# A drain of GpSimd between the third and the fourth half tile, and a count loaded behind the tiles in the text

## The chip, the cores and the metric

The kernel runs on one core of one Trainium2 chip. The metric is the device time of one execution in microseconds (us). Every run is one execution of the whole program; three runs of the kernel before were timed, and one more was taken with the hardware profiler.

## What is computed

`x` is [4, 3072, 256] in float32. The reference takes a Fourier transform over the sequence and then over the channels and keeps the real part. A channel mix follows on each token and its predecessor, and then a gated squared-ReLU layer; the 12288 tokens that come out go through a mixture of eight experts, of which each token takes one:

```python
X = np.fft.fft(np.fft.fft(x, axis=1), axis=2).real
xk = mu_k * X + (1 - mu_k) * X_prev;  xr = mu_r * X + (1 - mu_r) * X_prev
y = sigmoid(xr @ w_r) * (np.maximum(xk @ w_k, 0) ** 2 @ w_v)          # then 12288 tokens of 256
e_idx = argmax(y @ w_gate); gate_w = softmax(y @ w_gate)[e_idx]; eom = sigmoid(y @ w_output_gate)
for e in range(8):
    out[e_idx == e] = gate_w * eom[e] * (np.maximum(y @ w1[e], 0) @ w2[e])
```

## The kernel before

The first two thirds of the kernel (up to about 830 us of the span) do the Fourier transforms and the gated layer in 24 blocks of 512 tokens. For each block, GpSimd issues four indirect transfers that write the tokens' numbers into one list for each expert (`lists`, line 491).

Then comes the expert stage. It works in tiles of 256 tokens that all take the same expert, and in half tiles of 128 for what is left over of an expert. `make_plan` works out on the chip which expert each tile takes and where its list starts, and writes it into the table `plan`. `pipeline` walks a fixed sequence: 3 early tiles, 22 tiles and 5 half tiles (`HALVES`). A tile is gathered by an indirect transfer of GpSimd (`gather`, line 621, into `xg`), goes through the first product (`m1`, tile `hps`) and the second (`m2`, tile `o`), is scaled by ScalarE (line 706), and is written out by an indirect transfer of GpSimd (line 707, `out<-o,ix`): two stores for a tile, one for a half tile. GpSimd's queue is in order, so an instruction that waits there holds up every later transfer of GpSimd.

Behind the fixed sequence stands a branch (`tc.If(extra > 0)`, line 895) for inputs whose experts are so unevenly filled that more tiles are needed. Each of the five engines loads the count `extra` from `plan` into a register (line 890) and takes the branch by itself. In the profiled execution nothing is left over and every engine jumps over the code of the further tiles. On the path that is jumped to, each engine raises the semaphores that the skipped code would have raised; GpSimd does it for its eight transfer semaphores with one instruction, named INC_SWDGE_SEM in the profile. Then come the end of the program (line 926 in the profile): SyncE waits for all semaphores, GpSimd has a DRAIN, all engines meet at a barrier, the semaphores are cleared, and they meet again.

The instructions are not issued in the order of the text alone: a scheduler sets the order within each engine from dependencies and priorities, and `follow` adds an edge to it that carries no semaphore (`NoSync`).

Of the kernel before, what the change touches and what calls it, by code (L numbers as in the profile page):

```python
# [25 lines left out]
NTILE = NT // TT + E - 1  # L26
EARLY = 3
MORE = [22, 26, 31, 38, NTILE]
HALVES = 5
CAP = NT + TT  # L30
ROW = 265
FAR = 1 << 20
# [13 lines left out]
def constants():  # L46
# [28 lines left out]
    desc = np.broadcast_to(E - e8, (128, 4, E))  # L75
    base = np.broadcast_to(e8 * CAP, (128, 4, E))
    tri = np.broadcast_to((e8[:, None] >= e8[None, :]).astype(float), (128, E, E))
# [18 lines left out]
def moe_kernel(ctx: ExitStack, tc: tile.TileContext, x, mu_k, mu_r, wk2, wv2, wr2, wg, wo, w1, w2,  # L96
               c_f, c_t, c_m, c_r, c_s, c_id, out):
    nc = tc.nc
    PE, ACT, DVE, POOL, SP = nc.tensor, nc.scalar, nc.vector, nc.gpsimd, nc.sync
# [4 lines left out]
    def tt(o, a, b, op, eng=None):  # L104
        return (eng or DVE).tensor_tensor(out=o, in0=a, in1=b, op=op)  # L105

    def stt(o, a, s, b, op0, op1, **kw):
        return DVE.scalar_tensor_tensor(out=o, in0=a, scalar=s, in1=b, op0=op0, op1=op1, **kw)  # L108
# [26 lines left out]
    zeros = dram.tile([16, 4096], F32, name="zeros")  # L135
    lists = dram.tile([E * CAP + TT, 2], I32, name="lists")

# [14 lines left out]
    def follow(i, earlier, kind, reason):  # L152
        for k in earlier:
            tc.add_manual_dep(i.ins, k.ins.name, mybir.DependencyInfo(kind, mybir.DependencyReason.DATA), reason=reason)

    def load_later(o, i):
        follow(SP.dma_start(o, i), raws[1:2], mybir.DependencyClass.NoSync, "the first groups come first")
# [13 lines left out]
    def clear_lists():  # L171
        zero = bp.tile([128, 512], F32, name="zero", tag="lt", bufs=1)
        POOL.memset(zero, 0.0)
        load_later(zeros.rearrange("a (p d) -> (a p) d", d=512), zero)
        per = (E * CAP + TT) // (6 * 128) * 2
        far = bp.tile([128, per], I32, name="far", tag="lt", bufs=1)
# [239 lines left out]
    def tail_steps(n, vps, rs):  # L416
# [73 lines left out]
        for u in range(4):  # L490
            i = POOL.indirect_dma_start(lists[:, :], bass.IndirectOffsetOnAxis(ap=pi[:, u:u + 1], axis=0),  # L491
                                        cid[:, n, u], None,
                                        bounds_check=E * CAP - 1, oob_is_err=False)
            for k in done:
# [79 lines left out]

    c1 = {}
    weights, xtile, meta, index, chunks, regs = {}, {}, {}, {}, {}, {}
    hq, outs, stores = {}, {}, []

    def open_c1():
        sa.close()  # L580
# [17 lines left out]
    def width(t):  # L598
        return 2 if t < NTILE else 1

    def read_plan(t):
        why = "experts and list starts are clamped to their ranges, flags are 0 or 1"
        regs[t] = [nc.values_load_multi_w_load_instructions(
            c1["plan"][0:1, t, i:i + 1], engines=[mybir.EngineType.SP], min_val=0, max_val=hi,
            skip_runtime_bounds_check_because=why)[1][0] for i, hi in ((0, E - 1), (1, 1), (2, E * CAP))]

    def gather(t):
        if t < 0:
            start = (t + EARLY) * TT
            src = lists[start:start + TT]  # L610
        else:
            read_plan(t)
            src = lists[bass.ds(regs[t][2], 128 * width(t)), :]
        ix = bp.tile([128, 2, 2], I32, tag="ix", name="ix", bufs=8)
        after_scatters(SP.dma_start(ix[:, 0:width(t)], src.rearrange("(p u) o -> p u o", u=width(t))))
        index[t] = ix
        place[t] = len(place)
        xg = c1["xg"][place[t] % 4]
        for u in range(width(t)):
            nr = NT if t >= 0 else NT - 1024  # L620
            POOL.indirect_dma_start(xg[:, u], None, rows[0:nr],  # L621
                                    bass.IndirectOffsetOnAxis(ap=ix[:, u, 0:1], axis=0),
                                    bounds_check=nr - 1, oob_is_err=False)
# [14 lines left out]
    def split_w(t, c):  # L638
        h, l = weights[t][c // 2]
        k = slice((c % 2) * 512, (c % 2) * 512 + 512)  # L640
        split(h[:, k], l[:, k], c1["raw"][c // 2][:, k])
# [46 lines left out]
    def m2(t, p):  # L688
        if p == 0:
            outs[t] = [pm.tile([128, D], F32, tag="m", name=f"o{u}") for u in range(width(t))]  # L690
        h, l = hq.pop((t, p))
        for u in range(width(t)):
            for a in range(2):
                f = 2 * p + a
                wh, wl = weights[t][2 + f // 4]
                cols = slice((f % 4) * D, (f % 4) * D + D)
                tok = slice(u * 128, u * 128 + 128)
                ps = outs[t][u]
                PE.matmul(ps, h[:, a, tok], wh[:, cols], start=f == 0, stop=False)  # L699
                PE.matmul(ps, l[:, a, tok], wh[:, cols], start=False, stop=False)  # L700
                PE.matmul(ps, h[:, a, tok], wl[:, cols], start=False, stop=f == 7)  # L701
        if p == 3:
            sc, ix = meta.pop(t), index.pop(t)
            o = bp.tile([128, 2, D], F32, tag="t1", name="o", bufs=2)
            for u in range(width(t)):
                ACT.activation(out=o[:, u], in_=outs[t][u], func=ACTF.Copy, scale=sc[:, u])
                i = POOL.indirect_dma_start(out[:, :], bass.IndirectOffsetOnAxis(ap=ix[:, u, 1:2], axis=0),
                                            o[:, u], None, bounds_check=NT - 1, oob_is_err=False)
                for k in stores[-4:]:
                    tc.declare_no_dep(i.ins, k.ins, reason="every token is in one list once: rows are distinct")  # L710
                stores.append(i)
            outs.pop(t)
            weights.pop(t)

# [5 lines left out]
    def make_plan():  # L720
# [44 lines left out]
        DVE.tensor_scalar(lc, lc, float(TT), None, ALU.mult)  # L765
        stt(lc, et, float(CAP), lc, ALU.mult, ALU.add)
        stt(st, et, 0.5, early[:, :, 0:1].to_broadcast([128, NTILE, 1]), ALU.is_lt, ALU.mult)
# [28 lines left out]
        DVE.tensor_scalar(at[:, :, 0:1], cum[:, :, E - 1:E], float(-MORE[0]), 0.0, ALU.add, ALU.max)  # L796
        DVE.tensor_scalar(at[:, :, 1:2], cuh[:, :, E - 1:E], float(-HALVES), 0.0, ALU.add, ALU.max)
        tt(half[:, 0:1, 3:4], at[0:1, :, 0:1], at[0:1, :, 1:2], ALU.add)

    def pipeline(seq, ahead=0):  # L800
        n = len(seq)
        bank = 0
        for t in seq:
            banks[t] = bank = 0 if t < 0 else 1 - bank
        for i in range(ahead, min(3, n)):
            gather(seq[i])
        if not ahead:
            load_w(seq[0], True)
            for c in range(8):
                split_w(seq[0], c)  # L810
            prep_x(seq[0])
            prep_scale(seq[0])

        def needs_w(i):
            return i < n and not (seq[i] < 0)

        if needs_w(1):
            load_w(seq[1])
        steps = [(i, p) for i in range(n) for p in range(4)]
        for g in range(len(steps) + 2):  # L820
            if g < len(steps):
                i, p = steps[g]
                m1(seq[i], p)
            if g >= 2:
                m2(seq[steps[g - 2][0]], steps[g - 2][1])
            if g < len(steps) and i + 1 < n:
                with ExitStack() as es:
                    for k in marks:
                        es.enter_context(tc.issue_after(k.ins))
                    if needs_w(i + 1):  # L830
                        split_w(seq[i + 1], 2 * p)
                        split_w(seq[i + 1], 2 * p + 1)
                    else:
                        weights[seq[i + 1]] = weights[seq[i]]
                    if p == 2:
                        prep_x(seq[i + 1])
                    if p == 3 and seq[i] < 0:
                        prep_scale(seq[i])
                    if p == 2 and seq[i + 1] >= 0:
                        prep_scale(seq[i + 1])  # L840
                if p == 0 and i + 3 < n:
                    gather(seq[i + 3])
                if p == 3 and needs_w(i + 2):
                    load_w(seq[i + 2])
# [41 lines left out]
    for _ in tail:  # L886
        pass
    sb.close()
    make_plan()
    value = lambda i, top, why: nc.values_load(  # L890
        c1["plan"][0:1, i:i + 1, 3:4].rearrange("p a b -> p (a b)"), min_val=0, max_val=top,
        skip_runtime_bounds_check_because=why)
    extra = value(NTILE, NTILE + E, "what is left of sums that add up to at most NTILE and E")
    pipeline(list(range(-EARLY, MORE[0])) + list(range(NTILE, NTILE + HALVES)), EARLY)
    with tc.If(extra > 0):
        total = value(0, NTILE, "a sum of rounded counts that add up to at most NT")
        halves = value(NTILE + 1, E, "at most one half tile of each expert")
        with ExitStack() as rest:
            for a, b in zip(MORE, MORE[1:]):
                rest.enter_context(tc.If(total > a))  # L900
                pipeline(list(range(a, b)))
        with tc.If(halves > HALVES):
            pipeline(list(range(NTILE + HALVES, NTILE + E)))

# [25 lines left out]
```

## Time and profile before

| what | value |
|---|---|
| time, median of 3 runs | 1190.78 us (1190.38 to 1191.68) |
| the profiled execution's own time | 1189.58 us |
| span of the profiled execution, first to last instruction | 1187.8 us |
| TensorE busy | 1135.6 us (96% of the span) |
| GpSimd busy | 228.4 us (19%) |

The span is shorter than the execution's own time by 1.78 us, which lie outside the first and the last instruction. The busy times count instructions that an engine executes; register loads, branches, semaphore instructions and drains, which an engine's sequencer carries out, are not among them and are found only by their line. In the names of the views "POOLq" is GpSimd's queue (sequencer) and "POOL" the engine behind it, and so for the others.

### The profile page before, as it was taken

The numbers are of one execution on the slowest core, as the hardware profiler recorded it, in microseconds if no ns is written. First come the engines' busy times: TensorE is split into PE (matmuls) and PEld (weight loads), VectorE is DVE, ScalarE is ACT, GpSimd is POOL, SyncE is SP. The second block draws the span as 40 slices with busy tenths as digits, with TensorE's granted clock in tenths as the row PEclk, the third lists the DMA queues.
The fourth block names the chain that finished last, engine by engine and source line by source line (L and its number), as shares of the span: only waits on it lengthen the run. The fifth ranks groups of instructions, "written<-read, shape, count | busy, mean of one in ns | idle before, by whom it ended". The sixth has DMA issues, their size and how long they took to land.

```text
span 1187.8 us, 19728 instructions
## 1 busy us (share of the span) xinstructions
PE 1135.6 (96%) x6743; PEld 971.6 (82%) x6743; DVE 892.6 (75%) x2032; ACT 775.3 (65%) x1611; POOL 228.4 (19%) x228
## 2 busy tenths in 40 slices
PE   5499999999999999999999999999999999999994
PEld 1477888888888888888887888877999999999994
DVE  1899898578869768768857877776677777777782
ACT  3577777567777667767756666855376676667671
POOL 1000111111100111111111111123342433343220
PEclk9699999999999999999999999999999999999998
DMA  8753551214432215324100000202234133441580
GB/s 275 235 183 126 157 160 55 88 57 130 128 126 81 81 54 144 76 65 128 48 28 29 28 28 19 90 20 55 88 119 147 47 113 109 118 124 38 156 246 13
DMA packets 63176, 119.17 MB, mean 100 GB/s; under 512 B 14299, under 2 KB 41181, under 8 KB 62297
## 3 DMA queue, kind: packets, MB, share of 16 engines
q1 hardware_dynamic: 51015, 91.62, 25.2%
q0 software_dynamic: 9296, 16.76, 4.6%
q10 hardware_dynamic: 2754, 9.44, 2.8%
q8 instruction: 55, 0.90, 0.4%
q14 instruction: 56, 0.46, 0.2%
HBM read 116.43 MB, written 46.57 MB: 137 GB/s over the span
## 4 chain that ended last, share of the span: by engine, by line
PE 87%; DMA 3%; DVE 3%; issue 3%; ACT 1%; SPq 1%; POOL 0%; POOLq 0%; ACTq 0%
PE v L252 8%; PE v L253 7%; PE v L254 7%; PE psk L252 7%; PE psk L253 7%; PE psk L254 7%; PE hps L254 4%; PE hps L253 4%; PE hps L252 4%; PE o L701 4%; PE o L700 4%; PE o L699 4%; PE ps L364 4%; PE ps L252 2%; PE psr L252 2%
## 5 line engine op out<-in xcount | busy, mean ns | idle before, releaser
L491 POOL DMA_INDIRECT lists<-cid,pi x96 | 100.9, 1051 | 683.9 <-DVE pi L488 622.3
L108 DVE SCALAR_TENSOR_TENSOR t<-psk,t 128x512 f32<-128x512 f32 x192 | 132.3, 689 | 62.5 <-ACT t L530 60.3
L530 ACT ACTIVATE t<-psk 128x512 f32<-128x512 f32 x192 | 114.3, 597 | 97.6 <-PE psk L254 84.8
L105 DVE TENSOR_TENSOR ql<-t,qh 128x512 fp32r<-128x512 f32 x192 | 132.4, 690 | 37.0 <-ACT qh L102 35.2
L252 PE MATMUL psk<-kh,wkh 128*128 128x512 f32 x384 | 156.6, 408 | 2.2 <-DVE t L108 1.2
L252 PE MATMUL v<-qh,wvh 128*128 128x512 f32 x384 | 153.7, 400 | 0.2 <-ACT qh L102 0.2
L253 PE MATMUL v<-qh,wvl 128*128 128x512 f32 x384 | 152.0, 396 | 0.0
L253 PE MATMUL psk<-kh,wkl 128*128 128x512 f32 x384 | 151.6, 395 | 0.0
L254 PE MATMUL psk<-kl,wkh 128*128 128x512 f32 x384 | 151.1, 394 | 0.0
L254 PE MATMUL v<-ql,wvh 128*128 128x512 f32 x384 | 150.2, 395 | 0.0
L102 ACT ACTIVATE qh<-t 128x512 fp32r<-128x512 f32 x192 | 120.7, 629 | 42.3 <-DVE t L108 35.4
L684 ACT ACTIVATE hh<-hps 128x512 fp32r<-128x512 f32 (+1 forms) x120 | 67.4, 562 | 107.6 <-PE hps L254 89.9
L108 DVE SCALAR_TENSOR_TENSOR hl<-hps,hh 128x512 fp32r<-128x512 f32 (+1 forms) x120 | 77.5, 646 | 73.7 <-ACT hh L684 63.1
L621 POOL DMA_INDIRECT xg<-rows,ix x55 | 61.5, 1119 | 183.0 <-PE hps L254 48.1
L252 PEld LDWEIGHTS psk<-kh,wkh 128*128 128x128 f32 x384 | 72.5, 189 | 17.6 <-DVE t L108 1.6
L254 PEld LDWEIGHTS v<-ql,wvh 128*128 128x128 f32 x384 | 72.3, 188 | 17.2 <-DVE ql L105 0.4
L254 PEld LDWEIGHTS psk<-kl,wkh 128*128 128x128 f32 x384 | 72.3, 188 | 16.7
L252 PEld LDWEIGHTS v<-qh,wvh 128*128 128x128 f32 x384 | 72.3, 188 | 15.3 <-ACT qh L102 0.9
L253 PEld LDWEIGHTS psk<-kh,wkl 128*128 128x128 f32 x384 | 72.6, 189 | 14.2
L253 PEld LDWEIGHTS v<-qh,wvl 128*128 128x128 f32 x384 | 72.5, 189 | 14.3
L108 DVE SCALAR_TENSOR_TENSOR mx<-xt,omu,mx 128x512 f32<-128x512 f32 x96 | 71.9, 749 | 6.3 <-ACT mx L402 5.3
L105 DVE TENSOR_TENSOR wlb<-raw,whb 128x512 fp32r<-128x512 f32 x112 | 73.3, 686 | 2.5 <-ACT whb L102 0.8
(219 smaller groups left out, 3102.5 us busy)
## 6 DMA issues: line engine op xcount, KB each, us to landing
raw<-in_moe_w SPq DMA_DIRECT2D x112, 512.0 KB
rows<-row SPq DMA_DIRECT2D x24, 530.0 KB
raw<-scr SPq DMA_DIRECT2D x24, 512.0 KB
out<-zeros SPq DMA_DIRECT2D x48, 256.0 KB
xs<-in_x SPq DMA_DIRECT2D x24, 480.0 KB
scr<-e ACTq DMA_DIRECT2D x18, 480.0 KB
tb<-in_c_t SPq DMA_DIRECT2D x20, 256.0 KB
scr<-xs POOLq DMA_DIRECT2D x6, 480.0 KB
```

What stands on the lines that cost most here:

```text
L102: return ACT.activation(out=o, in_=i, func=ACTF.Copy, scale=scale)
L105: return (eng or DVE).tensor_tensor(out=o, in0=a, in1=b, op=op)
L108: return DVE.scalar_tensor_tensor(out=o, in0=a, scalar=s, in1=b, op0=op0, op1=op1, **kw)
L252: PE.matmul(ps, ah, bh, start=start, stop=False)
L253: PE.matmul(ps, al, bh, start=False, stop=False)
L254: return PE.matmul(ps, ah, bl, start=False, stop=stop)
L364: PE.matmul(ps[:, a * 128:a * 128 + 128], f[:, a, c, par * 128:par * 128 + 128], tb[:, a, c], start=c == 0, stop=c == 1)
L491: i = POOL.indirect_dma_start(lists[:, :], bass.IndirectOffsetOnAxis(ap=pi[:, u:u + 1], axis=0), cid[:, n, u], None, bounds_check=E * CAP ...
L530: ACT.activation(out=t, in_=ps, func=ACTF.Relu)
L621: POOL.indirect_dma_start(xg[:, u], None, rows[0:nr], bass.IndirectOffsetOnAxis(ap=ix[:, u, 0:1], axis=0), bounds_check=nr - 1, oob_is_err ...
L684: marks[:] = [last, ACT.activation(out=h, in_=ps, func=ACTF.Relu), stt(l, ps, 0.0, h.bitcast(F32), ALU.max, ALU.subtract)]
L699: PE.matmul(ps, h[:, a, tok], wh[:, cols], start=f == 0, stop=False)
```

## The change

A DRAIN of GpSimd is issued behind the store of the third of the five half tiles (`DRAIN_AT` is its number). Two edges hold it in its place in the order: it follows that store, and the stores of the fourth and fifth half tile follow it. The lines that load the count `extra` move behind the call of `pipeline` in the text.

```diff
+DRAIN_AT = NTILE + HALVES - 3
...
-    hq, outs, stores = {}, {}, []
+    hq, outs, stores, drains = {}, {}, [], []
...
                 stores.append(i)
+                if drains and t > DRAIN_AT:
+                    follow(i, drains[:1], mybir.DependencyClass.NoSync, "what is written from here on is retired at the end")
+            if t == DRAIN_AT:
+                drains.append(POOL.drain())
+                follow(drains[0], stores[-width(t):], mybir.DependencyClass.NoSync, "this much is retired first")
...
     make_plan()
+    pipeline(list(range(-EARLY, MORE[0])) + list(range(NTILE, NTILE + HALVES)), EARLY)
     value = lambda i, top, why: nc.values_load(
...
     extra = value(NTILE, NTILE + E, "what is left of sums that add up to at most NTILE and E")
-    pipeline(list(range(-EARLY, MORE[0])) + list(range(NTILE, NTILE + HALVES)), EARLY)
     with tc.If(extra > 0):
```

GpSimd's queue at the end of the expert stage, before: the last gather, the stores of the five half tiles, and the load of the count with its branch (drains are not among the rows that this listing shows).

```order
L621 DMA xg_8449<-rows,ix 128x265 [waits DMAHW0_49,DVE_49,PE_49]
L707 DMA out<-o,ix 12288x256 [waits DMASW0_49,Activation_49]
L707 DMA out<-o,ix 12288x256 [waits DMASW2_49,DMASW1_49,Activation_49]
L707 DMA out<-o,ix 12288x256 [waits DMASW3_49,Activation_49]
L707 DMA out<-o,ix 12288x256 [waits DMASW5_49,Activation_49]
L707 DMA out<-o,ix 12288x256 [waits DMASW6_49,DMASW4_49,Activation_49]
L890 TENSOR_LOAD plan [waits DVE_49]
L895 COMPARE_AND_BRANCH
```

The same place of GpSimd's queue after the change (line 708 is the store, 897 the load of the count).

```order
L622 DMA xg_8449<-rows,ix 128x265 [waits DMAHW0_49,DVE_49,PE_49]
L708 DMA out<-o,ix 12288x256 [waits DMASW0_49,Activation_49]
L708 DMA out<-o,ix 12288x256 [waits DMASW2_49,DMASW1_49,Activation_49]
L708 DMA out<-o,ix 12288x256 [waits DMASW3_49,Activation_49]
L708 DMA out<-o,ix 12288x256 [waits DMASW5_49,Activation_49]
L708 DMA out<-o,ix 12288x256 [waits DMASW6_49,DMASW4_49,Activation_49]
L897 TENSOR_LOAD plan [waits DVE_49]
L901 COMPARE_AND_BRANCH
```

Nothing that is listed has moved, and the waits are the same: the load of the count stood behind the last store before and stands there now. Between the fourth and the fifth of these rows (the stores of the third and of the fourth half tile) the built program now has the DRAIN, with no wait and no semaphore of its own. Instruction by instruction, that DRAIN is the one difference between the two programs on all five engines.

SyncE's queue at the same place, before: the last loads of weights and the load of the count.

```order
L633 DMA raw_8445<-in_moe_w 128x1024 [waits DMAHW2_49,DVE_49]
L633 DMA raw_8446<-in_moe_w 128x4x256 [waits DMAHW3_49,DVE_49]
L633 DMA raw_8447<-in_moe_w 128x4x256 [waits DMAHW4_49,DMAHW0_49,DVE_49]
L890 TENSOR_LOAD plan [waits DVE_49]
L895 COMPARE_AND_BRANCH
```

It reads the same after the change but for the line numbers, and so do the queues of TensorE, VectorE and ScalarE.

## Rows read from the trace of the kernel before

**Rows 1.** The page: span, and busy time, share and instructions of each engine.

```profile
span 1187.8 us, 19728 instructions
PE 1135.6 (96%) x6743; PEld 971.6 (82%) x6743; DVE 892.6 (75%) x2032; ACT 775.3 (65%) x1611; POOL 228.4 (19%) x228
```

**Rows 2.** Windows at the end: stretch, length, busy us of engines (instructions), clock, DMA share.

```profile
1158.00:1168.00 10.00, 10.00 (x90) 10.00 (x89) 6.21 (x16) 5.17 (x13) 1.96 (x2) 1.00 0.06 21
1168.00:1173.00 5.00, 3.19 (x28) 2.99 (x26) 0.42 (x1) 0.86 (x2) 0.98 (x1) 1.00 0.06 19
1173.00:1175.80 2.80, 0.00 (x0) 0.00 (x0) 0.00 (x0) 0.00 (x0) 0.00 (x0) 1.00 0.13 34
1178.20:1187.80 9.60, 0.00 (x0) 0.00 (x0) 0.00 (x0) 0.00 (x0) 0.00 (x0) 0.50 0.00 0
```

**Rows 3.** Line 895, branch and jumped-to path: count, min/median/max ns, first and last start.

```profile
L895 SPq EVENT_SEMAPHORE  x9: 17/17/17, 1159.7 to 1160.3; - x9
L895 POOLq EVENT_SEMAPHORE  x5: 17/42/43, 1175.2 to 1175.7; - x5
...
L895 POOLq COMPARE_BRANCH  x1: 53/53/53, 1172.3 to 1172.3; - x1
L895 POOLq INC_SWDGE_SEM  x1: 2335/2335/2335, 1175.8 to 1175.8; - x1
```

**Rows 4.** Line 926, the program's end, in three windows.

```profile
L926 SPq EVENT_SEMAPHORE  x7: 27/28/28, 1178.1 to 1178.5; - x7
L926 POOLq DRAIN  x1: 8812/8812/8812, 1178.2 to 1178.2; - x1
...
L926 SPq DRAIN  x2: 7/10/13, 1178.8 to 1178.9; - x2
...
L926 POOLq EVENT_SEMAPHORE  x2: 17/17/17, 1187.0 to 1187.1; - x2
...
L926 POOLq DRAIN  x2: 44/76/107, 1187.2 to 1187.5; - x2
```

**Rows 5.** Line 914, the program's start.

```profile
L914 POOLq INC_SWDGE_SEM  x1: 27/27/27, 0.1 to 0.1; - x1
...
L914 POOLq DRAIN  x1: 188/188/188, 0.3 to 0.3; - x1
```

**Rows 6.** GpSimd's transfers over the span, by tile: count, KB each.

```profile
scr<-xs POOLq DMA_DIRECT2D x6, 480.0 KB
...
lists<-cid,pi POOLq DMA_INDIRECT x96
xg<-rows,ix POOLq DMA_INDIRECT x55
out<-o,ix POOLq DMA_INDIRECT x55
...
scr<-xs POOLq DMA_DIRECT2D x1, 192.0 KB
```

**Rows 7.** Line 890, the load of the count: queue, ns, start.

```profile
L890 SPq TENSOR_LOAD <-plan x1: 273/273/273, 1155.4 to 1155.4; - x1
...
L890 POOLq TENSOR_LOAD <-plan x1: 498/498/498, 1171.7 to 1171.7; - x1
```

**Rows 8.** Timeline of GpSimd: start, us, what, idle before it and its releaser.

```profile
1158.09 0.98 POOL L707 DMA_INDIRECT out<-o,ix  x1 [7.44 <-ACT o L706]
1166.48 0.98 POOL L707 DMA_INDIRECT out<-o,ix  x1 [7.42 <-ACT o L706]
1171.97 0.98 POOL L707 DMA_INDIRECT out<-o,ix  x1 [4.51 <-ACT o L706]
```

**Rows 9.** GpSimd's transfer queue (q0): packets in 1160 to 1162, then in 1174 to 1175.

```profile
q0 software_dynamic: 2, 0.00, 0.1%
...
q0 software_dynamic: 5, 0.01, 5.5%
```

**Rows 10.** Timeline of VectorE behind the third store.

```profile
1158.36 0.69 DVE L105 TENSOR_TENSOR wlb<-raw,whb 128x512 fp32r<-128x512 f32 x1 [0.19 <-ACT whb L102]
...
1163.32 0.42 DVE L108 SCALAR_TENSOR_TENSOR hl<-hps,hh 128x256 fp32r<-128x256 f32 x1
1165.38 0.42 DVE L108 SCALAR_TENSOR_TENSOR hl<-hps,hh 128x256 fp32r<-128x256 f32 x1 [1.63 <-ACT hh L684]
```

**Rows 11.** Lines 491 and 707: GpSimd's indirect transfers, min/median/max ns.

```profile
L491 POOL DMA_INDIRECT lists<-cid,pi x96: 977/979/1576, 125.8 to 844.4; - x96
...
L707 POOL DMA_INDIRECT out<-o,ix x55: 978/1017/1472, 859.8 to 1172.0; - x55
```

## The prediction

> **What bounds the kernel now.** I read the page first. TensorE is busy for 1135.6 of 1187.8 us [rows 1], so over the body of the kernel it is the bound, and GpSimd with 228.4 us is far from it. A change that touches only GpSimd's queue can therefore matter only where TensorE has nothing left to do, and the windows at the end show that place [rows 2]: TensorE is full from 1158 to 1168 (10.00 of 10 us), ends in the next window, and from 1173 to 1187.8 no engine executes anything. These last 15 us or so, 1.2% of the span, are register, branch and semaphore work, which the busy times don't count; so I went on to the lines of the branch, the program's end and the program's start.
>
> The tail reads like this. GpSimd starts the fifth half tile's store at 1171.97 and has written its descriptors after 0.98 us [rows 8]; the last packets of its transfer queue fall in 1174 to 1175 [rows 9]. GpSimd's queue took the branch at 1172.3, and its first instruction at the target starts at 1175.2: five semaphore waits, then INC_SWDGE_SEM at 1175.8 for 2.335 us [rows 3]. At 1178.2 comes its DRAIN, which takes 8.812 us; the barrier follows at 1187.0, and all is over at 1187.8 [rows 4]. SyncE, released at 1178.1, is through its waits and drains by 1178.9 and has nothing to do for the 8 us that follow [rows 4]. So the chain that ends the program runs through one instruction that executes nothing visible.
>
> What does this DRAIN do? All of GpSimd's transfers have landed by 1175, and the engine behind the queue has been empty since 1172.95, so it waits for neither. At the program's start the same two instructions, on the same queue, take 27 ns (INC_SWDGE_SEM) and 188 ns (a DRAIN behind the first fills) [rows 5]; and right after the long DRAIN two more take 44 and 107 ns [rows 4]. What lies between the short ones and the long one is that GpSimd issued 6 + 1 + 96 + 55 + 55 = 213 transfers [rows 6] with no DRAIN among them. My reading, which is an inference, is bookkeeping: each issued transfer leaves an entry that somebody must clear, the DRAIN clears all since the last one, 8.812 / 213 = 41 ns each, and after that there is nothing to clear.
>
> [...]
>
> **The change, part by part.** *The load of the count.* This part does nothing. In the profile of before the load already runs behind the tiles: at 1155.4 us on SyncE, behind its last weight load, and at 1171.7 us on GpSimd, behind its last store [rows 7]. The built order of all five queues is the same before and after. Cost 0; the cover is not needed, since nothing moves.
>
> *The added DRAIN, at its place.* It stands in GpSimd's queue behind the third half tile's store, which starts at 1158.09 and is generated at 1159.07 [rows 8]. Behind it in the queue stand only the fourth store (1166.48), the fifth (1171.97), and the load of the count. Nobody else's work waits for GpSimd any more: the last gather is ahead of it. By the price above it has 6 + 1 + 96 + 55 + 53 = 211 entries to clear, 211 x 41 ns = 8.7 us. If it starts with the store's issue, it ends at 1158.1 + 8.7 = 1166.8; if it must first see the third store land (its last packets fall behind 1160 [rows 9]), at about 1160.5 + 8.7 = 1169.2. I take 1159.07 + 8.7 = 1167.8. The fourth store's data are ready at 1166.2, so that store waits some 1.6 us and is generated by 1169.1. That delay costs nothing: the fifth store can't start before ScalarE has scaled its half tile, which gives 1171.97. The cover is gone if the DRAIN ends later than 1171.97 - 1.28 (one store with its issue) = 1170.7. So the DRAIN may take up to 11.6 us from 1159.07 before it costs anything, and each us beyond is lost one for one.
>
> *The last DRAIN.* It now has two entries to clear, 0.08 us by the price above, and at least the 0.04 to 0.19 us of the short ones. It doesn't give back all of 8.8 us, because something else is late next: SyncE's waits and drains, which run from 1178.1 to 1178.9, beside the long DRAIN until now. The barrier can then start at 1178.95 instead of 1187.0, and with the 0.8 us that follow it [rows 4] the span would end at 1179.75: **-8.05 us**. Its bounds are 0 (the DRAIN costs the same whenever it is issued) and 8.05.
>
> *INC_SWDGE_SEM.* It is untouched, but it stands behind the same 213 transfers, and its 2.335 us against 27 ns at the start [rows 5] suggest that it too looks through what is not cleared yet (11 ns each). The one at the start raises no semaphores while this one raises eight, so the row of the start is not a price for it. SyncE raises its own with nine instructions between 1159.7 and 1160.3 [rows 3], about 0.075 us each; eight would be 0.6 us. Its new time lies between 0.03 and 2.335 us. I take 0.4, between 0.03 and 0.6, because with two entries left it is nearest to the rows with none: **-1.9 us**. It is the least certain term, with bounds 0 and -2.3.
>
> Nothing else takes its place: on the jumped-to path GpSimd is the last engine to arrive, and the landing of the last store (by 1175) and the 2.9 us between branch and target are as before.
>
> Sum: -8.05 - 1.9 = -9.95 us. The profiled execution, whose own time is 1189.58, would come to about 1179.6; it lies 1.2 us under the median of the runs shown, so the forecast for the median is 1190.78 - 9.95 = **1180.8 us**.
>
> **The rivals.**
>
> *Only the DRAIN gets shorter.* INC_SWDGE_SEM has its own reasons (eight semaphores) and stays at 2.3 us: 1190.78 - 8.05 = 1182.7. For it: the two rows of INC_SWDGE_SEM are not alike in what they raise. Against: 0.3 us for each raised semaphore is four times what SyncE pays.
>
> *The added DRAIN is held up, and the last store is late.* At its place VectorE works: from 1158.36 to 1163.74 almost without a gap, then 0.42 us in every two [rows 10]; the last DRAIN ran alone. GpSimd's transfers show what company can cost it: 0.98 us at best, 1.58 at worst, medians of 0.979 and 1.017 [rows 11]. With the worst factor, 1.6, the DRAIN takes 14.0 us and ends at 1173.1, and the fifth store starts 1.28 + 0.2 us later, at 1174.6: 2.6 us late, which gives 1183.4. If it stands still altogether until 1163.7 and then runs at four fifths, it ends at 1163.7 + 10.9 = 1174.6, the fifth store starts at 1176.1, 4.1 us late, and the time is 1184.9.
>
> [...]
>
> *No change.* The long DRAIN is a price of a drain at the end, or of what INC_SWDGE_SEM leaves behind, and not of the transfers before it; or the added one clears nothing. Then the added one is hidden and the last one is as long as ever: 1190.8. For it: the long one stands right behind an INC_SWDGE_SEM, and so does no other but the first. Against: the first DRAIN behind an INC_SWDGE_SEM took 188 ns.
>
> *Slower.* The added DRAIN blocks GpSimd's queue so long that the late last store eats all of the gain. It must then end 9.95 us behind 1170.7, at 1180.6, and so last 21.5 us from 1159.07, 2.4 times what the same work takes alone; at three times (26.2 us) the fifth store starts at 1186.7, 14.8 us late, and the time is 1195.6. Against it is that no transfer of GpSimd was stretched by more than 1.6.
>
> **How the numbers follow.** Forecast (both shrink): 0.50. Only the DRAIN: 0.20. Last store late by 1 to 5 us: 0.13. No change: 0.09. Slower: 0.05. The remaining 0.03 is for a gain of a part, from entries that only partly clear. The likeliest case has its own range of 1179.3 (INC_SWDGE_SEM at nothing, the runs' scatter of 0.6 beside it) to 1182.0. The range that holds the time 8 times in 10 takes in the two next cases: 1179.0 to 1185.5. A difference of 0.2% (2.4 us) is about what a measurement can tell from no change; faster by more is the first three cases and the rest, 0.86; the same 0.09; slower 0.05.
>
> **What the profile after would show.** The added DRAIN should stand on GpSimd's queue at about 1158 to 1159 and take 8 to 11 us; the fourth store should start at some 1168 instead of 1166.5 and the fifth at 1172.0 as before; INC_SWDGE_SEM should take under 0.7 us and the last DRAIN under 0.3; SyncE's waits, no longer hidden, should be what ends last ahead of the barrier; the span should be 1177.8. The prediction is wrong in its ground if the last DRAIN is still above 2 us, wrong in its cover if the fifth store starts after 1172.5, and wrong in one term if INC_SWDGE_SEM stays at 2.3.

## The result, and the profile after

The changed kernel takes 1180.38 us (median of 6 runs, 1178.75 to 1182.04) against 1190.73 us before (6 runs, 1190.38 to 1193.48): a ratio of 0.9909, with a 95% interval of 0.9896 to 0.9922. The 10.3 us are 0.9%, well above the 0.2% that a measurement can tell from no change. The forecast was 1180.8 us, in a range of 1179.0 to 1185.5.

The page after shows that no engine works noticeably less; what is gone is time in which none worked. TensorE's 1135.1 us were 1135.6, GpSimd's 228.8 were 228.4 [rows 1], and there is one instruction more.

```profile
span 1179.2 us, 19729 instructions
PE 1135.1 (96%) x6743; PEld 971.4 (82%) x6743; DVE 891.9 (76%) x2032; ACT 775.8 (66%) x1611; POOL 228.8 (19%) x228
```

The added DRAIN, found by its line (716), and the load of the count (897) on SyncE and GpSimd (count, min/median/max ns, first and last start):

```profile
L716 POOLq DRAIN  x1: 9873/9873/9873, 1159.4 to 1159.4; - x1
...
L897 SPq TENSOR_LOAD <-plan x1: 272/272/272, 1157.0 to 1157.0; - x1
...
L897 POOLq TENSOR_LOAD <-plan x1: 504/504/504, 1173.3 to 1173.3; - x1
```

The timeline of GpSimd, with the third, fourth and fifth half tile's store (start, us, what, idle before it and its releaser):

```profile
1159.67 0.98 POOL L708 DMA_INDIRECT out<-o,ix  x1 [7.44 <-ACT o L707]
1170.18 0.98 POOL L708 DMA_INDIRECT out<-o,ix  x1 [9.52 <-issue]
1173.56 0.98 POOL L708 DMA_INDIRECT out<-o,ix  x1 [2.40 <-ACT o L707]
```

And the tail: the branch (line 901) and the program's end (line 932).

```profile
L901 POOLq EVENT_SEMAPHORE  x5: 17/43/43, 1176.7 to 1177.3; - x5
...
L901 POOLq COMPARE_BRANCH  x1: 57/57/57, 1173.9 to 1173.9; - x1
L901 POOLq INC_SWDGE_SEM  x1: 240/240/240, 1177.4 to 1177.4; - x1
```

```profile
L932 SPq EVENT_SEMAPHORE  x14: 17/28/28, 1177.6 to 1179.2; - x14
L932 POOLq EVENT_SEMAPHORE  x4: 17/17/17, 1178.4 to 1179.1; - x4
L932 POOLq DRAIN  x3: 46/107/222, 1177.7 to 1178.9; - x3
L932 SPq DRAIN  x3: 7/7/13, 1178.3 to 1178.6; - x3
```

How to read it against the rows of before: the body of this execution runs about 1.6 us later (the third store starts at 1159.67, not 1158.09 [rows 8]), so the tails are best compared from that store on. It was 1187.8 - 1158.09 = 29.7 us to the end, and is 1179.2 - 1159.67 = 19.5. The fifth store starts 13.89 us behind the third, as before (13.88), although the fourth starts 10.51 us behind it instead of 8.39: it is no longer released by ScalarE, and the profile shows nothing that it waits for ("issue"). It stands behind the DRAIN, which ends at 1169.31, and no other engine waits for it. From the fifth store to INC_SWDGE_SEM it is 3.8 us both times [rows 3, 8]. Then INC_SWDGE_SEM takes 0.240 us instead of 2.335, and the longest of the three DRAINs at the end 0.222 instead of 8.812 [rows 4]. SyncE's waits and drains, from 1177.6 to 1178.4, are now what the barrier waits for.

### The profile page after: what moved, and what is told of

Same layout as the page of the kernel before. It is cut to its first block, busy times and chain, and to the rows that moved or that the text cites. A ratio compares the mean times of both kernels' runs of the same rounds, so it can differ in the third digit from the quotient of the medians.

```text
span 1179.2 us, 19729 instructions
## 1 busy us (share of the span) xinstructions
PE 1135.1 (96%) x6743; PEld 971.4 (82%) x6743; DVE 891.9 (76%) x2032; ACT 775.8 (66%) x1611; POOL 228.8 (19%) x228
## 4 chain that ended last, share of the span: by engine, by line
PE 88%; DVE 3%; DMA 3%; issue 3%; ACT 1%; SPq 1%; POOL 0%; POOLq 0%; ACTq 0%; DVEq 0%
PE v L253 8%; PE v L254 7%; PE v L255 7%; PE psk L253 7%; PE psk L254 7%; PE psk L255 7%; PE hps L255 4%; PE hps L253 4%; PE hps L254 4%; PE o L702 4%; PE o L701 4%; PE o L700 4%; PE ps L365 4%; PE psr L253 2%; PE ps L253 2%
## 5 line engine op out<-in xcount | busy, mean ns | idle before, releaser
L253 PE MATMUL hps<-xh,wha 128*128 128x256 f32 (+1 forms) x256 | 73.0, 285 | 2.8 <-DVE plan L801 1.7
```

Source lines behind the costliest of these rows:

```text
L253: PE.matmul(ps, ah, bh, start=start, stop=False)
```

## The experiments

The theory at the outset: every transfer that GpSimd issues leaves an entry, a DRAIN clears those that are left at a price for each, INC_SWDGE_SEM looks through them, and the change moves that work beside TensorE's last half tiles. The rivals: the price is fixed, it belongs to the program's end, it goes by bytes, the place of the count's load matters, or the added DRAIN isn't free at its place. Four kernels ran on one chip (before: 1188.47 us there), four on a second (1188.34) and three, once each, on a third (1190.01); each is compared with the kernel before on its own chip.

### The load of the count alone

The call of `pipeline` stands ahead of the load in the text, and there is no DRAIN.

```diff
     make_plan()
+    pipeline(list(range(-EARLY, MORE[0])) + list(range(NTILE, NTILE + HALVES)), EARLY)
     value = lambda i, top, why: nc.values_load(
...
-    pipeline(list(range(-EARLY, MORE[0])) + list(range(NTILE, NTILE + HALVES)), EARLY)
```

> The lines that load the count stand behind the pipeline, and there is no added DRAIN. My theory: the built order of all five queues is that of the kernel before, so this half of the change is worth nothing: 1190.7 us, the last DRAIN 8.8 us and INC_SWDGE_SEM 2.3 us. Rival (the load's place matters): part of the 10.3 us is gained, below 1188 us.

Measured: 1188.05 us, ratio 0.9997 (0.9987 to 1.0006). Its branch and end:

```profile
L895 POOLq INC_SWDGE_SEM  x1: 2335/2335/2335, 1174.3 to 1174.3; - x1
...
L926 POOLq DRAIN  x3: 44/107/8812, 1176.7 to 1186.1; - x3
```

Both instructions take what they took before, to the nanosecond. This half of the change is worth nothing; all of the gain is the DRAIN's.

### A DRAIN behind the lists instead

To the kernel before, one DRAIN behind the last transfer into the lists, and gathers of the tiles behind it.

```diff
         scatters[:] = done
+        if n == NB * 6 - 1:
+            ended.append(POOL.drain())
+            follow(ended[0], done, mybir.DependencyClass.NoSync, "the lists' transfers first")
...
+            if t >= 0:
+                follow(i, ended, mybir.DependencyClass.NoSync, "behind the drain")
```

> The kernel before with one DRAIN of GpSimd behind the last transfer into the lists, at about 845 us. Ahead of it 7 + 96 + 6 = 109 transfers are issued, behind it 104. My theory (every transfer since the last DRAIN costs it 41 ns, and INC_SWDGE_SEM 11 ns): the added one 4.5 us, plus the store ahead of it being generated, hidden in GpSimd's idle time; the last one 104 x 41 = 4.3 us; INC_SWDGE_SEM 1.1 to 1.4 us; time 1190.7 - 4.5 - 1.1 = 1185.1 us. Rival (the first long DRAIN of a program pays a fixed price, however many transfers): the added one 8.8 us, the last one under 0.3, time as after the change, 1180.4 us. Rival (a price of the end): last DRAIN 8.8 us, 1190.7 us.

Measured: 1188.38 us, ratio 1.0001 (0.9991 to 1.0011): neither 5.6 us nor 10.3 us of gain, but none. The added DRAIN (line 501), then the branch and the end, and from the timeline the last transfer ahead of the added one:

```profile
L501 POOLq DRAIN  x1: 12684/12684/12684, 843.5 to 843.5; - x1
...
L900 POOLq INC_SWDGE_SEM  x1: 2275/2275/2275, 1175.7 to 1175.7; - x1
...
L931 POOLq DRAIN  x3: 46/107/8552, 1178.0 to 1187.2; - x3
```

```profile
845.99 0.98 POOL L491 DMA_INDIRECT lists<-cid,pi  x1 [0.30 <-issue]
```

Here the theory breaks in its number. The last DRAIN has 104 transfers to clear and takes 8.552 us, 82 ns each, hardly less than the 8.812 us with 213. The DRAIN behind the lists works from the end of the last transfer (846.97) to 856.19, 9.2 us for 109 transfers, 85 ns each. Together the two clear 213 transfers in 17.8 us. If a transfer costs the same in the kernel before, where one DRAIN of 8.8 us comes at the end, about half of them must have been cleared there already, by something else. The same two numbers speak against a price for bytes or packets: up to the end of the added DRAIN GpSimd's transfer queue moved 4.04 MB in 4304 packets, and behind it 12.72 MB in 4992 packets, three times the bytes at nearly the same time for each transfer. A price of the end and a fixed price were not refuted by this run alone; the next ones do that.

### A DRAIN at both places

The changed kernel with the same lines.

> The changed kernel with a second DRAIN behind the last transfer into the lists. My theory: the DRAIN behind the third half tile has only 102 transfers to clear, 4.2 us and about 1 us until the store ahead of it is generated, so 5.2 us instead of 9.9; the fourth store is then not late; the time is that of the changed kernel, 1180.4 us, because the fourth store's delay cost nothing. Rival (the late fourth store does cost): 1 to 2 us faster than the changed kernel. Rival (fixed price): this DRAIN is either 9.9 us or nearly nothing.

Measured: 1178.06 us, ratio 0.9911 (0.9895 to 0.9928), as the changed kernel. The DRAIN behind the third half tile (line 721), the end, and that half tile's store:

```profile
L721 POOLq DRAIN  x1: 9612/9612/9612, 1156.7 to 1156.7; - x1
...
L906 POOLq INC_SWDGE_SEM  x1: 240/240/240, 1174.3 to 1174.3; - x1
...
L937 POOLq DRAIN  x3: 46/107/208, 1174.6 to 1175.9; - x3
```

```profile
1156.92 0.98 POOL L713 DMA_INDIRECT out<-o,ix  x1 [7.44 <-ACT o L712]
```

I had expected 5.2 us for it and got 9.6, against 9.87 in the changed kernel: with the lists' transfers cleared or not, it finds about the same amount, 102 here and hardly more there. The miss has the same cause as the one before. Here the number is known, since a DRAIN leaves nothing older to the next one (in the changed kernel the last, with two transfers behind the added one, takes 0.222 us): from the end of the store (1157.90) to its own end (1166.30) the DRAIN takes 8.40 us for 102 transfers, 82 ns each.

### More transfers that carry nothing

To the kernel before, four transfers of 32 bytes behind each block's transfers into the lists, to a tensor that nobody reads.

```diff
         scatters[:] = done
+        for u in range(4):
+            i = POOL.dma_start(tiny[4 * n + u:4 * n + u + 1], ident[0:1, 0:8])
+            follow(i, done, mybir.DependencyClass.NoSync, "behind the lists' transfers")
```

> The kernel before with 96 more transfers of GpSimd, four behind each block's transfers into the lists, each of 32 bytes from one partition to a scratch tensor that nobody reads; no added DRAIN. My theory (the price is for a transfer, whatever it moves): the last DRAIN clears 309 transfers, 12.8 us; INC_SWDGE_SEM 3.4 us; time 1190.7 + 4.0 + 1.1 = 1195.8 us. Rival (the price is for the bytes or packets moved, of which these have hardly any): last DRAIN 8.8 to 9.2 us, time 1190.7 to 1191.2 us.

Measured: 1186.49 us, ratio 0.9983 (0.9973 to 0.9993): 2 us less, with 96 transfers more. Both expectations missed.

```profile
L899 POOLq INC_SWDGE_SEM  x1: 1535/1535/1535, 1177.1 to 1177.1; - x1
...
L930 POOLq DRAIN  x3: 40/107/5545, 1178.6 to 1184.8; - x3
```

The last DRAIN is shorter, not longer. That fits no theory in which it clears all that was ever issued, and it fits one in which the older ones are cleared in batches: more transfers move the place of the last batch, and what is left at the end can be less. That is a reading so far; the last three runs below test it. The two instructions are 4.1 us shorter together and the kernel only 2.0, so some 2 us are lost elsewhere. In the profiled execution they lie ahead of the tail: from the third half tile's store to the end it takes 26.0 us against 29.75 with the load alone on the same chip, and that store starts at 1159.36 against 1156.59. Where in the body, is open.

### The DRAIN one half tile later, and one earlier

`DRAIN_AT` is `NTILE + HALVES - 2` or `- 4`; a third kernel is the changed one again.

> The added DRAIN stands behind the fourth half tile's store instead of the third's. My theory: it has 212 transfers to clear and starts 8.4 us later, so it ends 8.7 us behind the generation of the fourth store, about 4.4 us after the fifth store is ready; the fifth store is that much late and the time is 1180.4 + 4.4 = 1184.8 us, with INC_SWDGE_SEM and the last DRAIN as short as in the changed kernel. Rival (what is cleared is what has landed by itself in the meantime, and the place is free): 1180.4 us.

> The added DRAIN stands behind the second half tile's store, where VectorE is busy for 7.4 of 8 us. My theory: 210 transfers, 8.6 us behind the store's generation, so 9.8 us; the third store is about 1.4 us late, the fourth and fifth are not; time as the changed kernel, 1180.4 us. Rival (VectorE's work locks GpSimd out): the DRAIN takes 15 us or more, and the third store is 7 us late; the time is still about the same.

> The changed kernel once more, on the same chip as the two others of this call: 1180.4 us, for comparison.

Measured: behind the fourth 1182.55 us, ratio 0.9949 (0.9928 to 0.9969); behind the second 1177.55, 0.9898 (0.9881 to 0.9916); the changed kernel 1178.01, 0.9902 (0.9886 to 0.9919). Behind the fourth half tile, the DRAIN, the end, and the fourth and fifth store:

```profile
L716 POOLq DRAIN  x1: 9955/9955/9955, 1164.7 to 1164.7; - x1
...
L932 POOLq DRAIN  x3: 46/107/141, 1179.2 to 1180.5; - x3
```

```profile
1164.94 0.98 POOL L708 DMA_INDIRECT out<-o,ix  x1 [7.41 <-ACT o L707]
1175.55 0.98 POOL L708 DMA_INDIRECT out<-o,ix  x1 [9.63 <-issue]
```

The cover is real and has an end. The fifth store comes 10.61 us behind the fourth instead of 5.49 [rows 8], 5.1 us late, and the kernel loses 4.5 us of the gain (4.4 were expected). Behind the second half tile (DRAIN, the store ahead of it, and what VectorE does from the end of that store to the end of the DRAIN, in the column of 7.79):

```profile
L716 POOLq DRAIN  x1: 9793/9793/9793, 1149.0 to 1149.0; - x1
...
L932 POOLq DRAIN  x3: 46/107/304, 1175.3 to 1176.6; - x3
```

```profile
1149.24 0.99 POOL L708 DMA_INDIRECT out<-o,ix  x1 [3.45 <-ACT o L707]
...
1150.20:1158.80 8.60, 8.60 (x78) 8.60 (x77) 7.79 (x19) 6.62 (x16) 0.03 (x1) 1.00 0.72 233
```

With VectorE busy for 7.79 of 8.60 us the DRAIN takes 8.57 us behind the store's end (1150.23 to 1158.80); in the changed kernel VectorE is busy for 5.1 of 8.6 us, and it takes 8.66. It isn't held up. The two kernels differ by 0.4 us (1177.55 and 1178.01; their runs, 1175.85 to 1178.66 and 1175.55 to 1178.85, overlap almost wholly): between these two places there is nothing to choose, since the fifth store isn't late at either.

### The changed kernel with the transfers that carry nothing

> The changed kernel with the 96 more transfers of 32 bytes. My theory: the DRAIN behind the third half tile clears 307 transfers, 12.6 us and some 1.2 us ahead of that, so 13.8 us; it ends past the point where the fifth store begins to wait, and that store is about 1.3 us late: 1181.7 us; INC_SWDGE_SEM and the last DRAIN stay below 0.3 us. Rival (the price is for bytes): 9.9 us and 1180.4 us.

Measured: 1182.04 us, ratio 0.9944 (0.9926 to 0.9961).

```profile
L720 POOLq DRAIN  x1: 6602/6602/6602, 1156.8 to 1156.8; - x1
```

The time is near what I had expected, and that is luck, for the reason is another: the DRAIN takes 6.6 us, not 13.8, ends at 1163.4 and delays no store in the profiled execution. That execution took 1178.66 us and the three others 1181.4 to 1183.1. As in the run without the DRAIN, the added transfers cost some us elsewhere, and where is open.

### Where the older ones are cleared

Three kernels, one execution each, with a single added DRAIN at other places: behind the third tile, behind the twelfth (`DRAIN_AT = 2` and `11`), and, in the kernel before, behind the twelfth block of the first stage (`if n == 11` in the lines of the second experiment, with the next block's transfers into the lists behind it).

> The added DRAIN stands behind the third of the 22 tiles (number 2), with 135 transfers ahead of it and 78 behind. What the runs so far say: 81.5 ns for each transfer that is not cleared, and in the kernel before only 107 of 213 are left at the end, though a DRAIN behind the lists finds about all of the 109 up to there; so something clears the 106 oldest between the lists and the second half tile. If it does so at once, soon behind the lists (a full ring): this DRAIN finds 29 and takes 2.4 us from the end of the store ahead of it. If it clears one by one as new ones come (a sliding limit of about 107): 107 and 8.8 us. If it does so late: 135 and 11.1 us. The last DRAIN, with 78 behind the added one: 6.4 us, INC_SWDGE_SEM 1.75 us, time some 3 us below the kernel before.

> The added DRAIN stands behind the twelfth tile (number 11), with 171 transfers ahead of it and 42 behind. Cleared at once soon behind the lists: 65 found, 5.4 us from the end of the store ahead of it. Sliding limit: 107, 8.8 us. Late: 171, 14 us. The last DRAIN: 42 x 81.5 ns + 0.06 = 3.5 us, INC_SWDGE_SEM 1.04 us, time 6.6 us below the kernel before.

> The added DRAIN stands in the first stage, behind the twelfth block's transfers into the lists, with 55 transfers ahead of it and 158 behind. It finds 55: 4.5 us from the end of the transfer ahead of it. The last DRAIN tells what the clearing in between hangs on: a ring that fills again from empty clears about 106 at about the 161st to 170th transfer, so some 52 are left and the last DRAIN takes 4.3 us, INC_SWDGE_SEM 1.2 us; a sliding limit leaves 107, 8.8 us; no clearing leaves 158, 12.9 us.

Measured, against 1190.01 us: 1187.20, 1185.19 and 1184.48 us. Some 3 us less were expected of the first and 2.8 came; of the second 6.6, and 4.8 came. In the second the tail is as expected (22.9 us from the third half tile's store, 29.7 before), so the 1.8 us that are missing lie ahead of it, in one execution. Behind the third tile, with the store ahead of the DRAIN:

```profile
L716 POOLq DRAIN  x1: 8704/8704/8704, 911.0 to 911.0; - x1
...
L901 POOLq INC_SWDGE_SEM  x1: 1760/1760/1760, 1176.4 to 1176.4; - x1
...
L932 POOLq DRAIN  x3: 46/107/6429, 1178.1 to 1185.1; - x3
```

```profile
913.87 1.00 POOL L708 DMA_INDIRECT out<-o,ix  x1 [0.30 <-issue]
```

Behind the twelfth tile, with the store ahead of it:

```profile
L716 POOLq DRAIN  x1: 9272/9272/9272, 1017.9 to 1017.9; - x1
...
L901 POOLq INC_SWDGE_SEM  x1: 1040/1040/1040, 1178.0 to 1178.0; - x1
...
L932 POOLq DRAIN  x3: 46/107/3489, 1179.1 to 1183.1; - x3
```

```profile
1020.80 1.00 POOL L708 DMA_INDIRECT out<-o,ix  x1 [0.30 <-ACT xh L103]
```

Behind the twelfth block, with the transfer ahead of it:

```profile
L502 POOLq DRAIN  x1: 9202/9202/9202, 482.0 to 482.0; - x1
...
L899 POOLq INC_SWDGE_SEM  x1: 1240/1240/1240, 1176.3 to 1176.3; - x1
...
L930 POOLq DRAIN  x3: 46/107/4301, 1177.5 to 1182.4; - x3
```

```profile
484.54 1.36 POOL L491 DMA_INDIRECT lists<-cid,pi  x1 [0.30 <-issue]
```

The last DRAINs of the runs with a single added one give the price, since there nothing else runs. With 1, 2, 3, 42, 78 and 104 transfers left (behind the fourth, the third and the second half tile, the twelfth and the third tile, and the lists) they take 0.141, 0.222, 0.304, 3.489, 6.429 and 8.552 us: 0.06 us and **81.7 ns for each transfer that is left** ((8.552 - 0.141) / 103). INC_SWDGE_SEM, with 2, 42, 78 and 104, takes 0.240, 1.040, 1.760 and 2.275: 0.2 us and **20 ns each**. By both lines the kernel before has 107 left at its end. A price of the end, and a fixed one, are refuted. All of these are indirect transfers of 128 rows; what one of another shape costs, these lines don't tell.

The rest follows by counting. 213 - 107 = 106 had been cleared in the kernel before. The DRAIN behind the twelfth tile, with 171 issued, ends at 1027.19, 5.39 us behind its store, which is 65 transfers: again 106 had gone. The run with the DRAIN behind the twelfth block, which leaves 158 to come, has 4.301 us at the end, 52 transfers: 158 - 52 = 106. So in each of these runs 106 transfers had been cleared, counted from the last DRAIN, at no price that shows, and none while the last 42 of the kernel before were issued; a limit that slides would have left about 107 each time. That they go together, in one batch, is what the counts suggest and not a mechanism: no row shows the clearing itself or a ring that fills, and no run shows a second clearing of 106.

Two DRAINs in mid-kernel took longer than their entries. The one behind the third tile ended 4.8 us behind the last store, where 29 transfers are 2.4; 107 would have been 8.8 and 135 have been 11.1. The one behind the twelfth block ended at 491.16, 5.3 us behind the last transfer, where at most 55 can have been left, 4.6 us, and 4.5 were expected. In both, the last packets of GpSimd's queue fall late, at 917.95 and 488.15, some 3.1 and 2.3 us behind the end of the last transfer (1.1 us in the changed kernel), so a wait for them may be a part of it; no run separates that. A count from a DRAIN in mid-kernel is therefore an upper bound, and the counts at the end carry the argument. With the 96 small transfers, 309 - 67 = 242 were cleared (67 from the last DRAIN's 5.545 us), and 307 - 65 = 242 up to the DRAIN of 6.6 us, which 106 at a time doesn't give, so the number of transfers alone doesn't set how many go. The two long DRAINs and this count are open.

## Why the prediction was right, step by step

*The place.* Right: the gain comes whole from the 15 us in which no engine worked, and of these from two instructions on GpSimd's queue. From the third store on, the tail is 10.2 us shorter; the forecast was 9.95.

*The load of the count.* Right: 0, shown by the run with it alone (0.9997), and by the built order ahead of it.

*The price of clearing.* The step "8.812 / 213 = 41 ns each" and "211 entries to clear" is wrong in both factors: 105 are left at the third half tile, at 82 ns. A price for each transfer that is left holds, 81.7 ns over 1 to 104 of them, though what the DRAIN does with each no row shows; that the last DRAIN clears all that were ever issued does not hold. The product, 8.7 us, came out by luck: the DRAIN before (107 left) and the added one at its new place (105) meet almost the same remainder, 8.66 us from the store's end (1160.65) to 1169.3. Of the two choices in that step, the start at the end of the store's generation fits in the changed kernel and in the others with the DRAIN at or beside that place, best where the number is known (102 transfers, 8.40 us). Where the two factors matter, as behind the lists, the number fails: the forecast from it for that run was 5.6 us, and the run gave nothing.

*The cover.* Right: the DRAIN ended 8.66 us behind the end of the third store (8.7 forecast), the fourth store was 2.1 us late (1.6 forecast) and the fifth not at all. One half tile later the cover is gone, at 4.5 us.

*The last DRAIN.* Right: 8.05 us were forecast; it takes 0.222 us, less than SyncE's 0.8 us that run beside it, so that SyncE bounds the barrier, as said.

*INC_SWDGE_SEM.* Right in kind, and under-sized: 1.9 us were forecast and 2.1 came (2.335 to 0.240). Its price, too, was 20 ns for each of 107 and not 11 ns for each of 213. The rival "only the DRAIN gets shorter" falls with it.

*The rivals.* "No change" falls by the result, "last store late" and "slower" by the fifth store's 13.89 us. That a DRAIN stands still beside a busy VectorE isn't seen: from the end of the store ahead of it, it takes 8.57 us where VectorE is busy for 91% of the stretch, and 8.66 where it is busy for 60%. Nor is the last DRAIN's time a wait for GpSimd's engine: the engine's last instruction, the fifth store, ended at 1172.95 before [rows 8] and at 1174.54 after, and the DRAIN, which started at 1178.2 [rows 4] and at 1177.7, took 8.812 us and 0.222.

## What to carry to other kernels

Look at the stretch behind the last executed instruction by its lines, not by busy times: a program that ends with GpSimd's indirect transfers can have time there in two instructions that count as no work, here 11.1 us. A DRAIN of GpSimd issued while the bound engine still works, late enough that few transfers follow and early enough that it ends before the next store that matters, took 10.2 us off the tail here; the 81.7 ns for each uncleared transfer of this kind tell how early at the least. And a total divided by a count is a price only when a second point, with another count, lies on the same line: here it was the right total beside the end and the wrong price behind the lists and in mid-kernel.

## What had not been expected

By the counts, 106 of GpSimd's transfers had been cleared by something other than a DRAIN in each run of this kernel that can be counted, and this left no wait on its queue that a row shows. So, by this reading, the last DRAIN's length hangs on where the program stops behind such a clearing: 52 transfers and 4.3 us with the DRAIN behind the twelfth block, 107 and 8.8 us in the kernel before. And 96 more transfers made the kernel 0.17% faster (0.9973 to 0.9993), with the two instructions at the end 4.1 us shorter; that they moved the place of the last clearing is the likeliest reason, but how, the counts don't explain.
